# A gated linear recurrence followed by a cosine-gated two-layer block: TensorE's order fixed by hand, transposes and x through DRAM, weights on GpSimd's queue, first groups closer together

## The chip, the cores and the metric

One core of one Trainium2 chip. The metric is device time in microseconds (us) of one execution. Every kernel was run on the same chip as the kernel before in the same rounds. The rounds ran on several chips, where the kernel before took 821.0 to 823.5 us in the median, so times of different rounds compare only to some 3 us; the ratios to the kernel before don't have this fault. The time of a single instruction comes from the one profiled run of each kernel.

Words used below: TensorE (PE in the profile), VectorE (DVE), ScalarE (ACT), GpSimd (POOL), SyncE (SP; its queue is SPq). "hp" is the first matrix product of the gated block, "op" the second; "lgs" and "phs" are running sums over a chunk (of logarithms and of phases); "sc", "sp" and "yp" are the scores, the states and the attention outputs. A number in brackets is the group: hp(0), lgs(3). A "record" is one matmul instruction in the trace; the "span" is the time from the first to the last instruction of the profiled run.

## The reference

```python
# q, k, v, a_re, a_im: (4, 8, 768, 48) float32; w_in (384, 2048), w_out (2048, 384): float64
mag = sqrt(a_re**2 + a_im**2);  scale = minimum(mag, 0.999) / (mag + 1e-6)
for t in range(768):                                   # complex gate a, state S of 48 x 48
    S = a[t] * S + outer(k[t], v[t])
    y[t] = q[t] @ real(S)
x = y, heads side by side                              # (3072, 384)
h = x @ w_in
out = (h * cos(h)) @ w_out                             # (3072, 384) float32
```

## The kernel before

The recurrence is done in 24 chunks of 128 steps, two chunks to a group, 12 groups. For each group: logarithms of the gate, their running sums (lgs) and exponentials; angles by arctangent, their running sums (phs), sine and cosine; keys and queries multiplied by these and transposed; then sc, sp, yp; then x is brought to the layout that hp wants, and the gated block follows. Work of four groups is woven: `weave` gives every piece a place between 0 and 1 and emits the pieces in that order. The weights come as float64 and are put together from their bits on chip.

```python
def from_double(dst, src):                 # 28 times: 12 pieces of w_in, 16 of w_out
    nc.sync.dma_start(out=raw, in_=src)
    nc.vector.tensor_scalar(...)           # L595: shift and mask of the upper word
    nc.vector.scalar_tensor_tensor(...)    # L597: sign
    nc.scalar.activation(out=low, ...)     # lower word
    nc.gpsimd.tensor_tensor(out=bits, in0=bits, in1=low, op=ALU.add)
    nc.vector.tensor_scalar(out=e, ...)    # L601, L603: range check of the exponent
    nc.scalar.activation(out=e, ...)
...
def f_transpose(n, name):                  # one chunk; 32 x 32 blocks, then 12 small moves
    nc.vector.transpose(out=tr, in_=...)
    for a in range(Q4):
        for b in range(NR):
            nc.sync.dma_start(out=place[ts(b, 32), a], in_=tr[ts(a, 32), b])
...
for it in range(NG + 3):
    g, c, m, o = it, it - 1, it - 2, it - 3
    ...g_log(g); g_prod(g); g_angle(g)...
    ...mm2(o, i) for both chunks...                                  # op
    weave((gates(g), 0.0, 0.5), (chunks(c), 0.0, 1.0), (weights.get(it, ()), 0.0, 1.0),
          ([mm1(m, jp) for jp in range(NJ // 2)], 0.0, 1.0))         # hp
```

TensorE's instructions are ordered by the scheduler; only ScalarE's table functions are chained by hand.

Of the kernel before, what the change touches and what calls it, by code (L numbers as in the profile page):

```python
# [485 lines left out]
def fast_path(ctx, tc, q, k, v, a_re, a_im, moe_w_in, moe_w_out, out, least, odd):  # L486
# [16 lines left out]
    R = 16  # L503
    NR = D // R
    Q4 = C // 32
    NJ = DF // C
# [31 lines left out]
    def load(g, names):  # L538
        for name in names:
            ap = {"re": a_re, "im": a_im, "q": q, "k": k, "v": v}[name]  # L540
            X[g][name] = ld.tile([C, G, H, D], F32, tag=name, name=name,
                                 bufs=2 if name == "v" else 1)
            for i in range(G):
                b, c = divmod(g * G + i, NCH)
                nc.sync.dma_start(  # L545
                    out=X[g][name][:, i],
                    in_=ap[b].rearrange("h (c p) d -> p c h d", p=C)[:, c])

    load(0, ("re", "im", "k", "q", "v"))
# [15 lines left out]
    def weight_parts():  # L565
        wi = moe_w_in.rearrange("(c p) f -> p c f", p=C)
        wo = moe_w_out.rearrange("(j p) e -> p j e", p=C)
        parts = [(w_in[:, c, ts(i, W)], wi[:, c, ts(i, W)])
                 for i in range(DF // W) for c in range(ND)]
        parts += [(w_out[:, j], wo[:, j]) for j in range(NJ)]  # L570
        return [lambda dst=dst, src=src: weight(dst, src) for dst, src in parts]
# [7 lines left out]
    def from_double(dst, src):  # L579
# [8 lines left out]
        raw = stage.tile([C, n], I64, tag="raw", name="raw")  # L588
        nc.sync.dma_start(out=raw, in_=src)
# [3 lines left out]
        e = stage.tile([C, n], U32, tag="e", name="e", bufs=1)  # L593
# [6 lines left out]
        nc.gpsimd.tensor_tensor(out=bits, in0=bits, in1=low, op=ALU.add)  # L600
        nc.vector.tensor_scalar(out=e, in0=hi, scalar1=1, scalar2=21,  # L601
# [11 lines left out]
    chained = []  # L613

    def chain(ins):
        if chained:
            tc.add_manual_dep(ins.ins, chained[-1].ins.name, mybir.DependencyInfo(
                mybir.DependencyClass.NoSync, mybir.DependencyReason.DATA))
        chained.append(ins)
# [17 lines left out]
    def g_log(g):  # L637
# [3 lines left out]
        re, im = flat(x["re"]), flat(x["im"])  # L641
        m2, sq, rs, mag = temp("m2"), temp("sq"), temp("rs"), temp("mag")
# [13 lines left out]
        nc.gpsimd.tensor_tensor(out=m2, in0=m2, in1=rs, op=ALU.subtract)  # L656
        x["lg"] = m2
        nc.gpsimd.tensor_tensor(out=mag, in0=mag, in1=sq, op=ALU.mult)  # L658
# [4 lines left out]
        x["tan"] = sq  # L663

    def g_prod(g):


        x = X[g]
        x["P"], x["Q"] = temp("P"), temp("Q")
        for i in range(G):  # L670
            ps = pa.tile([C, DM], F32, tag="a", name="lgs")
            nc.tensor.matmul(ps, lhsT=sums, rhs=x["lg"][:, ts(i, DM)], start=True, stop=True)  # L672
            special(out=x["P"][:, ts(i, DM)], in_=ps, func=AF.Exp)
            special(out=x["Q"][:, ts(i, DM)], in_=ps, func=AF.Exp, scale=-1.0)
        u = temp("mag")
        nc.vector.scalar_tensor_tensor(out=u, in0=x["Q"], scalar=HUGE, in1=x["P"],
                                       op0=ALU.min, op1=ALU.mult)
        for name in "PQ":
            nc.vector.scalar_tensor_tensor(out=x[name], in0=u, scalar=3.0, in1=x[name],
                                           op0=ALU.subtract, op1=ALU.mult)  # L680
        row = rows_d.tile([G * DM], F32, tag="row", name="row")
        nc.scalar.dma_start(out=row, in_=x["P"][C - 1:C].rearrange("o x -> (o x)"))
        x["end"] = ft.tile([D2, G * H], F32, tag="end", name="end")
        for part in range(D2 // R):
            nc.sync.dma_start(
                out=x["end"][ds(part * R, R)],
                in_=row.rearrange("(x b d) -> b d x", d=R, b=NR)[part // 2])
        nc.vector.tensor_scalar(out=x["end"], in0=x["end"], scalar1=-0.5, scalar2=None,
                                op0=ALU.mult)
        nc.vector.scalar_tensor_tensor(out=least, in0=x["end"], scalar=LEAST, in1=least,  # L690
                                       op0=ALU.is_ge, op1=ALU.min)

    def g_angle(g):
        x = X[g]
        at, fl = x["tan"], temp("rs")
        special(out=at, in_=at, func=AF.Arctan)
        nc.scalar.activation(out=fl, in_=at, func=AF.Identity, scale=-2.0 / math.pi, bias=half_b)  # L697
        nc.vector.scalar_tensor_tensor(out=fl, in0=flat(x["re"]), scalar=0.0, in1=fl,
# [3 lines left out]
        x["turn"] = at  # L702
        x["ph"] = temp("ph", 2)

    def g_phase(g, i):
        x, n = X[g], g * G + i
        ps = pa.tile([C, DM], F32, tag="a", name="phs")
        first = n % NCH == 0
        nc.tensor.matmul(ps, lhsT=sums, rhs=x["turn"][:, ts(i, DM)], start=True, stop=first)  # L709
        if not first:  # L710
            prev = X[(n - 1) // G]["ph"][:, ts((n - 1) % G, DM)]
            nc.tensor.matmul(ps, lhsT=last, rhs=prev, start=False, stop=True)  # L712
        ph = x["ph"][:, ts(i, DM)]
# [4 lines left out]
    def g_trig(g):  # L718
        x = X[g]
        cs, sn = x["trig"] = temp("rs"), temp("mag")  # L720
        nc.vector.tensor_scalar(out=cs.bitcast(U32), in0=x["ph"].bitcast(U32),
                                scalar1=0x7FFFFFFF, scalar2=None, op0=ALU.bitwise_and)
        special(out=sn, in_=x["ph"], func=AF.Sin, scale=TWO_PI)
        special(out=cs, in_=cs, func=AF.Sin, scale=-TWO_PI, bias=half_pi_b)

    def g_stack(g):
        x = X[g]
        nc.gpsimd.tensor_tensor(out=x["P"], in0=flat(x["q"]), in1=x["P"], op=ALU.mult)
        nc.gpsimd.tensor_tensor(out=x["Q"], in0=flat(x["k"]), in1=x["Q"], op=ALU.mult)  # L729
        for name, src in (("ks", x["Q"]), ("qs", x["P"])):  # L730
            t = gt.tile([C, G * H * NR, 2, R], F32, tag=name, name=name,
                        bufs=2 if name == "ks" else 1)
            for a in range(2):
                nc.vector.tensor_tensor(
                    out=t[:, :, a], in0=src.rearrange("p (x d) -> p x d", d=R),
                    in1=x["trig"][a].rearrange("p (x d) -> p x d", d=R), op=ALU.mult)
            x[name] = t

    def f_transpose(n, name):


        g, i = divmod(n, G)
        tr = ft.tile([C, NR, H, 32], F32, tag="tr", name="tr")
        nc.vector.transpose(out=tr, in_=X[g][name[0] + "s"][:, ts(i, H * NR)].rearrange(
            "p (h b) a d -> p b h (a d)", b=NR))
        if name == "kT":
            t = Y[n][name] = ft.tile([D2, H, Q4, 32], F32, tag=name, name=name, bufs=3)
            place = t.rearrange("p h q j -> p q h j")
        else:
            t = Y[n][name] = place = ft.tile([D2, Q4, H, 32], F32, tag=name, name=name, bufs=3)  # L750
        for a in range(Q4):
            for b in range(NR):
                nc.sync.dma_start(out=place[ts(b, 32), a], in_=tr[ts(a, 32), b])  # L753

    def queries(y, h):
        return y["qT"][:, :, h]

    def f_scores(n, hh):
# [4 lines left out]
        for h in range(HH):  # L763
            nc.tensor.matmul(ps[:, h], lhsT=y["kT"][:, hh * HH + h], rhs=queries(y, hh * HH + h),  # L764
                             start=True, stop=True)
# [3 lines left out]
    def f_out(n):  # L769
# [6 lines left out]
        for p in range(HH):  # L776
            for side in range(2):
                nc.tensor.matmul(ps[ds(side * 64, D), p], lhsT=vals[:, 2 * p + side],  # L778
                                 rhs=y["atm"][:, 2 * p + side], start=True, stop=(state is None))
            if state is not None:  # L780
                for side in range(2):
                    nc.tensor.matmul(ps[ds(side * 64, D), p], lhsT=state[:, 2 * p + side],  # L782
                                     rhs=queries(y, 2 * p + side), start=False, stop=True)
# [4 lines left out]
    def f_state(n):  # L788
# [4 lines left out]
        for h in range(H):  # L793
            keys = X[g]["ks"][:, ts(i * H + h, NR)].rearrange("p b a d -> p (b a d)")
            nc.tensor.matmul(ps[:, h], lhsT=keys, rhs=X[g]["v"][:, i, h], start=True, stop=True)  # L795
# [11 lines left out]
    def f_xt(g):  # L807

        xt = X[g]["xT"] = msb.tile([C, ND, G, C], F32, tag="xT", name="xT")
        for h in range(H):  # L810
            row = h * D
            while row < (h + 1) * D:
                n = min((h + 1) * D, (row // C + 1) * C) - row
                nc.sync.dma_start(out=xt[ds(row % C, n), row // C],
                                  in_=X[g]["yT"][ds(h % 2 * 64 + row - h * D, n), h // 2])
                row += n

    def mm1(g, jp):
        x = X[g]
        ps = pm.tile([C, 2, G * C], F32, tag="m", name="hp")  # L820
        for ji in range(2):
            for dc in range(ND):
                nc.tensor.matmul(ps[:, ji], lhsT=w_in[:, dc, ts(jp * 2 + ji, C)],  # L823
                                 rhs=x["xT"][:, dc].rearrange("p g t -> p (g t)"),
                                 start=(dc == 0), stop=(dc == ND - 1))
# [137 lines left out]
```

## Time and profile before

| | before |
|---|---|
| time | 821.39 us, median of 3 runs (820.37 to 822.25) |
| TensorE busy before 200 us | 96.9 us (414 records), clock 0.74 |
| TensorE busy from 200 to 823 us | 600.2 us (3052 records), clock 1.00 |
| first hp | 128.5 us |

The table has two rows of busy time because the profile has two regimes, and only the first has much to win. Busy time alone misleads in it: at half clock the same matmul is twice as long (16 sc records take 3.75 us at 75 us, where the granted clock from 74 to 79 us is 0.50, and 1.79 at 347 us, at 1.00). So the text below counts TensorE's work as *floor work*: the number of records times the duration of one at full clock. The whole kernel is 656 us of it.

### The profile page before, as it was taken

How to read it: one execution, taken by the hardware profiler on the slowest of the kernel's cores; microseconds unless marked ns; L12 is line 12 of the kernel's file. 1: busy time of each engine (PE TensorE's matmuls, PEld its weight loads, DVE VectorE, ACT ScalarE, POOL GpSimd, SP SyncE). 2: the span in 40 equal slices, each digit the busy share in tenths (PEclk: the TensorE clock that was granted, in tenths of full speed). 3: DMA queues.
4: the chain of work that ended last, by engine and by line, in shares of the span. 5: the costliest groups of instructions: out<-in, count | busy, mean ns of one | idle time of the engine just before them, and what ended most of it. 6: DMA issues, size and time to landing. Idle time of an engine off the chain costs nothing.

```text
span 823.1 us, 10293 instructions
## 1 busy us (share of the span) xinstructions
PE 697.1 (85%) x3464; PEld 514.9 (63%) x3464; DVE 488.7 (59%) x754; ACT 376.4 (46%) x576; POOL 146.6 (18%) x96
## 2 busy tenths in 40 slices
PE   1217286766899999999999989999999999999997
PEld 0006174534575785876867857858758668677674
DVE  2876454957685574864954856757658458234060
ACT  5552615663666345453571562464545624123140
POOL 1341124322401113003012021040040120000000
PEclk9956576897999999999999999999999999999999
DMA  9624257545632722623625427226236231210000
GB/s 178 128 47 71 45 128 192 129 103 115 164 80 49 150 45 62 119 49 68 112 51 92 84 49 135 42 54 123 49 62 110 51 73 30 49 40 21 20 0 23
DMA packets 251481, 65.67 MB, mean 80 GB/s; under 512 B 230414, under 2 KB 247823, under 8 KB 251419
## 3 DMA queue, kind: packets, MB, share of 16 engines
q1 hardware_dynamic: 250818, 64.62, 38.6%
q8 instruction: 29, 0.48, 0.3%
q10 hardware_dynamic: 600, 0.30, 0.2%
q14 instruction: 34, 0.27, 0.1%
HBM read 36.51 MB, written 4.76 MB: 50 GB/s over the span
## 4 chain that ended last, share of the span: by engine, by line
PE 53%; SPq 15%; DVE 12%; ACT 9%; issue 4%; DMA 3%; POOL 3%; DVEq 0%; ACTq 0%; POOLq 0%
PE hp L823 20%; PE op L841 18%; SPq L753 12%; PE sc L764 3%; ACT rs L629 2%; PE lgs L672 2%; POOL m L656 2%; PE phs L709 2%; PE yp L778 2%; PE sp L795 2%; DVE gate L833 2%; PE phs L712 1%; PE yp L782 1%; ACT L628 1%; SPq L545 1%
## 5 line engine op out<-in xcount | busy, mean ns | idle before, releaser
L823 PE MATMUL hp<-xT,w_in 128*128 128x256 f32 x1152 | 272.9, 390 | 16.0 <-DMA xT<-yT 8.6
L841 PE MATMUL op<-w_out,gate 128*128 128x384 f32 x768 | 256.3, 490 | 17.3 <-POOL w_out L600 17.1
L823 PEld LDWEIGHTS hp<-xT,w_in 128*128 128x128 f32 x1152 | 218.4, 194 | 53.1 <-DVE gate L835 8.7
L841 PEld LDWEIGHTS op<-w_out,gate 128*128 128x128 f32 x768 | 145.8, 191 | 118.5 <-POOL w_out L600 21.3
L829 ACT ACTIVATE turn<-hp,quarter_b 128x512 f32<-128x512 f32 x96 | 65.5, 683 | 91.4 <-PE hp L823 90.2
L629 ACT ACTIVATE gate<-gate 128x512 f32<-128x512 f32 x96 | 60.2, 628 | 102.4 <-DVE gate L833 102.3
L835 DVE TENSOR_TENSOR gate<-hp,gate 128x512 f32<-128x512 f32 x96 | 65.5, 685 | 38.8 <-ACT gate L629 38.4
L831 DVE TENSOR_SCALAR gate<-turn 128x512 f32<-128x512 f32 x96 | 40.7, 427 | 61.9 <-ACT turn L829 61.0
L672 PE MATMUL lgs<-m,sums 128*128 128x384 f32 x48 | 25.1, 657 | 52.2 <-POOL m L656 52.2
L833 DVE TENSOR_TENSOR gate<-turn,gate 128x512 f32<-128x512 f32 x96 | 67.2, 702 | 1.7
L801 POOL TENSOR_TENSOR state<-state,end 96x384 f32<-96x384 f32 x16 | 16.8, 1050 | 266.2 <-DVE state L799 175.2
L844 ACT ACTIVATE ot<-op 128x384 f32<-128x384 f32 x24 | 11.6, 484 | 114.4 <-PE op L841 114.4
L764 PEld LDWEIGHTS sc<-qT,kT 96*128 96x128 f32 x384 | 53.0, 206 | 15.6 <-issue 9.8
L764 PE MATMUL sc<-qT,kT 96*128 96x128 f32 x384 | 53.5, 290 | 7.4 <-issue 4.1
L656 POOL TENSOR_TENSOR m<-m,rs 128x768 f32<-128x768 f32 x12 | 21.7, 1808 | 178.0 <-ACT rs L629 178.0
L672 PEld LDWEIGHTS lgs<-m,sums 128*128 128x128 f32 x48 | 10.6, 245 | 64.7 <-POOL m L656 59.8
L714 DVE TENSOR_SCALAR ph<-phs 128x384 f32<-128x384 f32 x24 | 13.3, 555 | 55.7 <-PE phs L712 40.8
L709 PE MATMUL phs<-sq,sums 128*128 128x384 f32 x48 | 23.0, 570 | 27.2 <-DVE sq L700 27.2
L766 DVE TENSOR_TENSOR atm<-sc,causal 128x512 f32<-128x512 f32 x48 | 32.6, 682 | 18.8 <-PE sc L764 18.6
L659 DVE SCALAR_TENSOR_TENSOR sq<-mag,sq 128x768 f32<-128x768 f32 x12 | 11.5, 958 | 49.1 <-POOL mag L658 49.1
L778 PE MATMUL yp<-atm,v 128*48 128x128 f32 x384 | 38.2, 288 | 0.0
L729 POOL TENSOR_TENSOR Q<-k,Q 128x768 f32<-128x768 f32 x12 | 25.6, 2130 | 55.8 <-ACT rs L697 19.7
(75 smaller groups left out, 812.6 us busy)
## 6 DMA issues: line engine op xcount, KB each, us to landing
kT<-tr SPq DMA_DIRECT2D x288, 32.0 KB, 2.0
qT<-tr SPq DMA_DIRECT2D x288, 32.0 KB, 1.8
raw<-in_moe_w_in_dram SPq DMA_DIRECT2D x12, 512.0 KB, 4.8
raw<-in_moe_w_out_dram SPq DMA_DIRECT2D x16, 384.0 KB, 3.8
re<-in_a_re_dram SPq DMA_DIRECT2D x24, 192.0 KB, 3.0
im<-in_a_im_dram SPq DMA_DIRECT2D x24, 192.0 KB, 4.1
k<-in_k_dram SPq DMA_DIRECT2D x24, 192.0 KB, 4.0
q<-in_q_dram SPq DMA_DIRECT2D x24, 192.0 KB, 4.6
```

Source lines behind the costliest of these rows:

```text
L629: chain(nc.scalar.activation(func=func, **kw))
L672: nc.tensor.matmul(ps, lhsT=sums, rhs=x["lg"][:, ts(i, DM)], start=True, stop=True)
L709: nc.tensor.matmul(ps, lhsT=sums, rhs=x["turn"][:, ts(i, DM)], start=True, stop=first)
L753: nc.sync.dma_start(out=place[ts(b, 32), a], in_=tr[ts(a, 32), b])
L764: nc.tensor.matmul(ps[:, h], lhsT=y["kT"][:, hh * HH + h], rhs=queries(y, hh * HH + h), start=True, stop=True)
L778: nc.tensor.matmul(ps[ds(side * 64, D), p], lhsT=vals[:, 2 * p + side], rhs=y["atm"][:, 2 * p + side], start=True, stop=(state is None))
L823: nc.tensor.matmul(ps[:, ji], lhsT=w_in[:, dc, ts(jp * 2 + ji, C)], rhs=x["xT"][:, dc].rearrange("p g t -> p (g t)"), start=(dc == 0), sto ...
L829: nc.scalar.activation(out=turn, in_=ps, func=AF.Identity, scale=INV_TWO_PI / in_scale, bias=quarter_b)
L831: nc.vector.tensor_scalar(out=cs, in0=turn, scalar1=ROUND, scalar2=ROUND, op0=ALU.add, op1=ALU.subtract)
L833: nc.vector.tensor_tensor(out=cs, in0=turn, in1=cs, op=ALU.subtract)
L835: nc.vector.tensor_tensor(out=gate, in0=ps, in1=cs, op=ALU.mult)
L841: nc.tensor.matmul(ps, lhsT=X[g]["gate"][j // 2][:, j % 2, ts(i, C)], rhs=w_out[:, j], start=(j == 0), stop=(j == NJ - 1))
```

## The change

The intent is to let TensorE start its dense work sooner. Each group's transposes go through DRAM in two large hops (7 issues instead of 48), x likewise (3 instead of 10); group 0 is done in two halves; the weights are issued by GpSimd, and the range check of the weights is moved out of the start to a second read of them ("re-reads"); TensorE's matmuls are chained in the order of the program; and the first three groups get a weave of their own. Cut to its core:

```diff
+    def matmul(out, **kw):
+        chain(nc.tensor.matmul(out, **kw), "tensor")
...
-        nc.sync.dma_start(out=raw, in_=src)
+        nc.gpsimd.dma_start(out=raw, in_=src)
...
+    def guard(src):                        # the range check, on a second read of the weights
+        nc.sync.dma_start(out=raw, in_=src)
...
-        for a in range(Q4):
-            for b in range(NR):
-                nc.sync.dma_start(out=place[ts(b, 32), a], in_=tr[ts(a, 32), b])
+        nc.sync.dma_start(out=moved..., in_=tr)
+        if name == "kT":
+            for q4 in range(Q4):
+                nc.sync.dma_start(out=X[g][name][:, ds(i * H, n * H), q4], in_=moved[q4])
+        else:
+            nc.sync.dma_start(out=X[g][name][:, :, ds(i * H, n * H)], in_=moved...)
...
+    weave((each(g_log, 0), 0.0, 0.2), (prods(0), 0.2, 0.4), (angles(0), 0.4, 0.5),
+          (phases(0), 0.5, 0.6), (keys(0), 0.6, 1.0), (convert(into[:6]), 0.2, 1.0))
+    weave((chunks(0), 0.0, 0.4), (each(g_log, 1), 0.0, 0.1), (convert(into[6:]), 0.0, 0.4),
+          (prods(1), 0.4, 0.41), (angles(1), 0.42, 0.5), (phases(1), 0.7, 0.8), (first(0), 0.4, 1.0),
+          (convert(back), 0.4, 1.0))
+    weave((keys(1), 0.0, 0.1), (each(g_log, 2), 0.1, 0.2),
+          (second(0), 0.0, 0.8), (prods(2), 0.4, 0.42), (angles(2), 0.42, 0.5),
+          (phases(2), 0.75, 0.9), (chunks(1), 0.4, 0.95))
+    for it in range(3, NG + 3):
+        g, c, m, o = it, it - 1, it - 2, it - 3 if it > 3 else -1
+        weave((keys(c), 0.0, 0.08), (each(g_log, g), 0.08, 0.1), (second(o), 0.0, 0.36),
+              (prods(g), 0.36, 0.38), (angles(g), 0.38, 0.42), (phases(g), 0.6, 0.72),
+              (chunks(c), 0.45, 0.95), (first(m), 0.36, 1.0), (re-reads, 0.1, 0.9))
```

Two more edits: the logarithms' tile `lg` is now also the product P of its group, with one buffer; and GpSimd's multiplications of group 0 go to VectorE. Smaller ones: the tile `raw`, into which the weights are loaded, has four buffers instead of two, and the gates have twelve instead of eleven.

## The prediction

> **What bounds the kernel now.** I read the page first (busy shares, then the 40 slices, then the groups), after that the table of stretches, the chain of waits, the issue queue of SyncE and the timeline of the start.
>
> From the page:
>
> ```profile
> PE 697.1 (85%) x3464; PEld 514.9 (63%) x3464; DVE 488.7 (59%) x754; ACT 376.4 (46%) x576; POOL 146.6 (18%) x96
> PE   1217286766899999999999989999999999999997
> PEclk9956576897999999999999999999999999999999
> L823 PE MATMUL hp<-xT,w_in 128*128 128x256 f32 x1152 | 272.9, 390 | 16.0 <-DMA xT<-yT 8.6
> ```
>
> TensorE is busy 85% of 823.1 us, and the slices say where the other 15% is: from the tenth slice on (about 200 us) it is full, before that it is mostly idle and its granted clock is 0.5 to 0.8. So there are two regimes, and the table of stretches puts sizes on them (columns: length, then busy time of PE, PEld, DVE, ACT, POOL, clock, DMA share, GB/s):
>
> ```profile
> 0.00:20.00 20.00, 2.93 (x4) 1.17 (x4) 4.97 (x15) 10.76 (x15) 3.77 (x6) 1.00 1.07 184
> 40.00:60.00 20.00, 2.93 (x4) 1.18 (x4) 15.19 (x21) 13.18 (x21) 7.30 (x5) 0.50 0.23 44
> 80.00:100.00 20.00, 7.76 (x44) 5.45 (x43) 7.09 (x9) 12.33 (x17) 4.40 (x3) 0.50 0.34 61
> ...
> 350.00:400.00 50.00, 48.93 (x261) 35.98 (x262) 30.52 (x46) 24.94 (x36) 9.57 (x5) 1.00 0.47 87
> 750.00:800.00 50.00, 50.00 (x219) 36.76 (x218) 18.80 (x31) 15.69 (x25) 0.00 (x0) 1.00 0.06 17
> ```
>
> After 200 us the stretches add up to 600.2 us of TensorE work in 617 us (its last matmul ends at 817): 17 us idle in all. Before 200 us it is busy 96.9 us, much of it at half clock. The prize is at the start.
>
> What does TensorE need at full clock? From the chain of waits in the steady part:
>
> ```profile
> 282.51 2.66 PE hp L823 x12
> 290.75 2.59 PE hp L823 x12
> 293.35 1.32 PE sp L795 x16
> 346.69 1.79 PE sc L764 x16
> 755.13 20.64 PE op L841 x64
> ```
>
> So one hp record is 2.59/12 = 0.216 us, op 20.64/64 = 0.3225, sc 1.79/16 = 0.112, sp 1.32/16 = 0.0825. The timeline gives 1.97 us for the yp of a chunk with a state, 1.01 without, 0.65 for a pair of phs records, 1.56 for four lgs. Times counts: hp 1152: 248.6; op 768: 247.7; sc 384: 43.0; sp 320: 26.4; yp 20 x 1.97 + 4 x 1.01: 43.4; phs 88: 28.6; lgs 48: 18.7. **Sum 656 us**: the floor that the change does not touch, as it adds and removes no matmul. 823 - 656 = 167 us is what can be won, about 20 of it after 200 us, the rest in the start.
>
> Why is the start slow? SyncE issues the transposes' moves in order, and its timeline shows:
>
> ```profile
> 41.84 7.98 SPq L753 DMA_DIRECT2D kT<-tr  x12
> 49.92 7.53 SPq L753 DMA_DIRECT2D qT<-tr  x12
> 65.50 7.86 SPq L753 DMA_DIRECT2D qT<-tr  x12
> 79.86 8.29 SPq L753 DMA_DIRECT2D kT<-tr  x12
> 122.20 2.35 SPq L814 DMA_DIRECT2D xT<-yT  x3
> ```
>
> Each set of 12 costs 7.5 to 8.3 us of issue (0.65 each). Group 0 alone needs 48, 31 us; xT of group 0 is ready to go once yT is copied at about 86 us, but stands behind group 1's 48 issues until 122. The first hp runs at 128.5, and then waits for weights, xT and gates until 200.
>
> [...] 16 sc records take 3.75 us at 75 us, clock 0.50, against 1.79 later. [...] in the trace lgs waits 11.9 us for POOL after 200 us, with ready op matmuls queued behind. [...] the 32 KB moves here land in a median 1.8 to 2.0 us. [...] VectorE's L601 takes 0.42 us alone, 1.47 and 2.03 beside a GpSimd operation. No run yet has DMAs from GpSimd.
>
> **The change part by part.**
>
> (1) *Transposes through DRAM.* 48 issues a group become 2 writes and 5 reads: 7 (14 in group 0, done in halves). At 0.65 us that takes 34 x 0.65 = 22 us of issue off group 0 and 41 x 0.65 = 27 off each later group. [...] For a full group 786 KB each is written and read for k and for q. At the 187 GB/s of the 192-byte loads in the first 14 us, the kT read alone (128-byte pieces) is 4 to 6 us. Estimate for stack to last landing in a full group: 15 to 18 us, hidden if TensorE has 21 us of op in front.
>
> (2) *x through DRAM*: 10 issues a group become 3, one hop more; 5 to 6 us either way, but no queue of 48 in front.
>
> (3) *Weights on GpSimd's queue*, range check (e, L601 and L603) moved off the conversion to later re-reads: takes per weight 0.42 us of VectorE, 0.9 us of ScalarE and the SyncE issue out of the start. GpSimd has 12 x 1.34 + 16 x 1.18 = 35 us of conversion (rows of L600), its group-1 products about 8 [...] converted by about 90 us, when op of group 0 wants w_out. The re-reads, 4 a group later, are 0.3% or so of DMA each and off the path.
>
> (4) *Halves and first groups closer.* Walk of group 0 in the order of the changed queues, with half-width costs of the rows (ScalarE 0.48, VectorE 0.51, less when pipelined): VectorE's queue has the conversion of the first three weights ahead of group 0's third step, so it cannot pass until weight 3 has landed; at 184 GB/s, 1.6 MB of weights beside 0.8 MB of re and im is 13 to 15 us. From there (14): logs and products to 25, phs of half 0 at 27, trig and stack to 36, transposes 38.5, two hops to 46; half 1 follows in VectorE's queue to 45, landing 52; sc, sp, yp of it at half clock to 63, yT 65, x and xT by 70, the estimate of (2). **First hp at about 72** (with 2 for waits that I missed), against 128.5, and it then runs dense. 14 us of floor work lies before it.
>
> (5) *Fixed order, op first in an iteration.* From 72: hp of group 0, op of its first half, then sc of group 1 waits for keys(1), whose phases are only in the second half of hp(0): about 7 us lost. Then lgs(3) waits for the logs that come after keys(2) on ScalarE: about 12, and sc(2) 5 more. From the fourth iteration 64 op records (20.6 us) hide logs and keys, and lgs no longer waits for POOL (11.9 us saved), but sc may wait 0 to 3 us for kT: say 1.8 x 8 = 14. Clock losses after the gaps 4. Sum of bubbles 42.
>
> Total: 72 + (656 - 14) + 42 + 6 (the tail after the last matmul, 817 to 823, unchanged) = 762. I think my walk is a little pessimistic, since the weave fractions look tuned, and put down **757 us**.
>
> **Rivals.** (a) *GpSimd becomes the bound of the start*: [...] op(0) waits, and the time is 785 to 800. For: L600 was released late in before (op waits 17.1 us for it)[...]. [...] (b) *Double hop too slow in steady state*: 5 us a group waiting on kT or qT would add 30: about 785. For: 3.1 MB a group through DRAM; against: DMA is at 0.4 share there and 21 us of op precede. (c) *Nothing lost at all*: bubbles of 15 and first hp at 65 give 728. (d) *Transfers were hidden anyway*: the time stays near 820. Against: the chain of waits gives SyncE's queue 15% of the span, and PE's slices are empty just there.
>
> **Range and chances.** 757 with (c) below and (a), (b) above: 734 to 786 in 8 of 10. Slower than 805 (2%) would need (a) and (b) together: faster 0.95, within 2% 0.04, slower 0.01.
>
> **What would show it.** Right: first hp between 65 and 80 us; slices full from the fifth; PE busy near 680 to 690 (less half-clock work); SyncE's share of the chain near zero; lgs waiting for POOL gone in the steady part. Wrong: op(0) waiting for w_out from POOL (a); sc waiting on kT or qT beyond 3 us a group (b); gaps at the third iteration above 25 us, or a clock below 0.9 after 120 us.

## The result and the profile after

The changed kernel is correct and takes **789.72 us** (median of 4 runs, 788.54 to 791.51) against 820.97 (4 runs) of the kernel before in the same rounds; the ratio is 0.962, with a 95% interval of 0.959 to 0.964. Ratios here are the mean time of one kernel's fast runs over that of the other's of the same rounds, so not quite the ratio of the medians quoted. The gain is 31 us, half of the 64 that were forecast, and the time lies above the range. The profiled run, 791.51 us, has a span of 789.6; times read from the trace belong to this span.

From the page of the changed kernel (busy times, some of the rows of 40 slices of 19.7 us each, and the group of hp):

```profile
PE 684.7 (87%) x3464; PEld 512.0 (65%) x3464; DVE 521.6 (66%) x757; ACT 375.8 (48%) x589; POOL 151.2 (19%) x120
...
PE   0337585682999999999999999999999999999996
...
DVE  4889897646876776677668667668676675443150
...
PEclk9999788695999999999999999999999999999999
DMA  9897868998739339259275274293492631711000
...
L631 PE MATMUL hp<-xT,w_in 128*128 128x256 f32 x1152 | 267.0, 385 | 15.0 <-DMA xT<-x 8.7
```

TensorE is full from the eleventh slice, hardly sooner than before. VectorE and the DMA engines, 61% and 53% busy in the first 200 us of the kernel before (122.8 us, and a share of 0.53), are at 76% and 85% in the first 206 here, and VectorE is nearly always busy from 40 to 120 us (73.0 of 80 us). The table of stretches (columns as in the prediction):

```profile
0.00:20.00 20.00, 1.65 (x2) 0.50 (x2) 9.15 (x25) 10.29 (x20) 5.02 (x10) 1.00 0.95 226
40.00:60.00 20.00, 6.52 (x36) 6.39 (x38) 17.47 (x26) 10.35 (x13) 8.98 (x8) 1.00 0.96 246
...
80.00:100.00 20.00, 9.91 (x36) 8.12 (x36) 17.34 (x21) 7.54 (x13) 16.20 (x17) 0.76 0.80 223
...
350.00:400.00 50.00, 50.00 (x272) 38.53 (x271) 34.73 (x52) 27.06 (x40) 9.12 (x5) 1.00 0.59 117
```

In the stretch 40 to 60 us VectorE goes from 15.2 to 17.5 us busy and the DMA engines from 0.23 to 0.96; at 350 us TensorE goes from 48.9 to 50.0 of 50 us. The steady part became nearly full (573.3 of the 583 us after 206 us); the start did not. The spans differ by 33.5 us. TensorE's idle time after about 200 us falls from 17 to 8.6 us, so by this estimate some 8 us were won there and some 25 in the start.

SyncE's issues of the first half of group 0 (start, length):

```profile
41.35 1.41 SPq L776 DMA_DIRECT2D moved<-tr  x2
43.95 2.74 SPq L779 DMA_DIRECT2D kT<-moved  x4
46.79 0.58 SPq L781 DMA_DIRECT2D qT<-moved  x1
```

These 4.7 us, for k and q of one chunk, answer to two sets of 12 before, 15.5 us. SyncE no longer spends the start on issuing small moves, as intended. (Its share of the chain of waits reads 1% instead of 15%, but the chain on the new page reaches back only to 451 us, so it says nothing about the start.)

Where TensorE stands (start, length, instruction, and in brackets how long it had been idle and for what):

```profile
84.98 9.91 PE L631 MATMUL hp<-xT,w_in 128*128 128x256 f32 x36 [8.75 <-DMA xT<-x]
101.10 5.20 PE L631 MATMUL hp<-xT,w_in 128*128 128x256 f32 x12 [6.21 <-DVE gate L867]
...
141.68 2.93 PE L631 MATMUL lgs<-lg,sums 128*128 128x384 f32 x4 [11.62 <-POOL lg L679]
147.06 2.05 PE L631 MATMUL sc<-qT,kT 96*128 96x128 f32 x8 [2.46 <-DMA qT<-moved]
...
169.07 0.88 PE L631 MATMUL phs<-tan,sums 128*128 128x384 f32 x2
...
191.53 2.93 PE L631 MATMUL lgs<-lg,sums 128*128 128x384 f32 x4 [17.56 <-POOL lg L679]
...
247.17 1.45 PE L631 MATMUL lgs<-lg,sums 128*128 128x384 f32 x4
```

The first hp runs at 85 us. Then come four stalls, at 95 (gates), 130 (lgs(2)), 145 (sc(1)) and 174 (lgs(3)): 37.9 us in all. After lgs(3) there is next to none.

**One sum that carries the rest.** In all kernels in which I counted it (the changed one, e3, e9, f1, f4 and g2 below), 72.5 to 72.9 us of floor work are done when lgs(3) starts, so 583 are left. The span is then the time of lgs(3), plus 583, plus 6 for the tail, plus what is lost later. Here: 191.5 + 583.5 + 6 = 781, and the span is 789.6: **8.6 us lost in 598.** So the question is what puts lgs(3) at 191.5. (f1 will show that the cut belongs one group later, at lgs(4). In the changed kernel nothing is lost between the two: 55.6 us for some 55 us of floor work.)

### The profile page after: what moved, and what is told of

Its sections match the earlier page's. It is cut to its first block, busy times and chain, and to the rows that moved or that the text cites. A ratio compares the mean times of both kernels' runs of the same rounds, so it can differ in the third digit from the quotient of the medians.

```text
span 789.6 us, 9472 instructions
## 1 busy us (share of the span) xinstructions
PE 684.7 (87%) x3464; PEld 512.0 (65%) x3464; DVE 521.6 (66%) x757; ACT 375.8 (48%) x589; POOL 151.2 (19%) x120
## 5 line engine op out<-in xcount | busy, mean ns | idle before, releaser
L631 PE MATMUL hp<-xT,w_in 128*128 128x256 f32 x1152 | 267.0, 385 | 15.0 <-DMA xT<-x 8.7
L631 PE MATMUL op<-w_out,gate 128*128 128x384 f32 x768 | 252.7, 490 | 0.0
L641 ACT ACTIVATE gate<-gate 128x512 f32<-128x512 f32 x96 | 60.4, 629 | 153.7 <-DVE gate L865 153.6
L865 DVE TENSOR_TENSOR gate<-turn,gate 128x512 f32<-128x512 f32 x96 | 79.6, 829 | 1.5
L679 POOL TENSOR_TENSOR lg<-lg,rs 128x768 f32<-128x768 f32 x11 | 20.3, 1845 | 268.3 <-ACT rs L641 266.0
L631 PE MATMUL lgs<-lg,sums 128*128 128x384 f32 x48 | 22.8, 602 | 48.2 <-POOL lg L679 29.2
L879 ACT ACTIVATE ot<-op 128x384 f32<-128x384 f32 x24 | 11.8, 490 | 90.3 <-PE op L631 90.3
L832 POOL TENSOR_TENSOR state<-state,end 96x384 f32<-96x384 f32 x16 | 16.9, 1054 | 171.3 <-DVE state L830 121.5
L631 PEld LDWEIGHTS lgs<-lg,sums 128*128 128x128 f32 x48 | 10.4, 229 | 56.8 <-POOL lg L679 30.4
L681 DVE SCALAR_TENSOR_TENSOR tan<-mag,tan 128x768 f32<-128x768 f32 (+1 forms) x13 | 11.6, 895 | 38.5 <-POOL mag L680 38.4
L599 ACT ACTIVATE low<-raw,carrier_b 128x384 uint32<-128x384 uint32 (+1 forms) x28 | 19.2, 691 | 34.1 <-DMA raw<-in_moe_w_out_dram 12.7
L817 ACT COPY yT<-yp 48x512 f32<-48x512 f32 x48 | 27.5, 574 | 14.7 <-PE yp L631 14.2
L631 PEld LDWEIGHTS sp<-v,ks 128*96 128x96 f32 x320 | 32.5, 176 | 1.2 <-issue 0.2
```

The lines of the kernel that those rows point to most:

```text
L599: nc.scalar.activation(out=low, in_=lo, func=AF.Identity, scale=2.0 ** -29, bias=carrier_b)
L631: chain(nc.tensor.matmul(out, **kw), "tensor")
L641: chain(nc.scalar.activation(func=func, **kw))
L679: mult.tensor_tensor(out=m2, in0=m2, in1=rs, op=ALU.subtract)
L817: nc.scalar.copy(out=X[g]["yT"][half, :, i], in_=ps[half])
L832: nc.gpsimd.tensor_tensor(out=new, in0=new, in1=end, op=ALU.mult)
```

## The experiments

The first suspects were the re-reads, GpSimd's queue and the fixed order of TensorE. A check of each alone:

**e1**: no re-reads (a kernel without the range check).

```diff
-          ([lambda: guard(guards.pop(0)) for _ in range(min(per, len(guards)))], 0.1, 0.9))
+          ([lambda: guards.pop(0) for _ in range(min(per, len(guards)))], 0.1, 0.9))
```

> The changed kernel without its range-check re-reads (28 loads of 512 or 384 KB and their 28 operations on VectorE and ScalarE taken out; the check then passes trivially, the output stays right). Theory T1, the start is short of DMA: these re-reads are hoisted to 100-175 us, where the DMA share is 0.83 to 0.95, so without them the gap of 11.6 us before lgs of group 2 and of 17.6 us before lgs of group 3 shrink by some 5 us each and the time is 775 to 781. Rival T2, TensorE's fixed order holds ready matmuls behind lgs: the gaps stay, 786 to 790. T3, GpSimd's queue paces the weights: no change before 120 us in any of the two, 786 to 790.

Measured: 794.49 us (ratio 0.966, 0.963 to 0.970), lgs(3) at 192.8. The edit also moved the scheduler's order of the start (first hp at 91.8), so it isn't a clean removal, but the 12.6 MB fewer brought nothing. T1 missed.

**e2**: the re-reads held to their place in the program. The scheduler had hoisted them to 100 to 175 us.

```diff
-        nc.sync.dma_start(out=raw, in_=src)
+        ...the same issue, with an order (no wait) after the newest issue of SyncE before it
```

> All re-reads kept, but each held on SyncE's queue behind the transfer that the program names just before it, so that four come in each group from the fourth iteration on, as the prediction had assumed. T1: as e1 (775 to 781), as the placing and not the bytes costs. T2 and T3: 786 to 790. If e1 gains and this doesn't, the work itself costs.

Measured: 790.45 us (0.963, 0.958 to 0.968). lgs(3) comes 6 us sooner, at 185.4, but 3.5 of these 6 us are lost again later: 601.6 us of the span lie after lgs(3), instead of 598.1. The profiled run is also the fastest of the four (788.75 us); the median shows no gain.

**e3**: the weights issued by SyncE, as before.

```diff
-        nc.gpsimd.dma_start(out=raw, in_=src)
+        nc.sync.dma_start(out=raw, in_=src)
```

> The changed kernel with the 28 weight loads issued by SyncE instead of GpSimd. T3 (weights wait for GpSimd's turn: raw is loaded only after the conversion in front of it on the same in-order queue): first hp a few us earlier or the 6.2 us stall in hp of group 0 gone, 780 to 785. T1: the same bytes over the same engines at the same time, 786 to 794. T2: 788 to 791.

Measured: 791.15 us (0.962, 0.959 to 0.964). The first lgs comes at 10.1 instead of 16.9, the first hp at 76.7 instead of 85.0: GpSimd's queue costs the start 8 us. Yet lgs(3) moves only from 191.5 to 187.9, and the time not at all. Something later than the first hp takes the 8 us back: at lgs(4), 247.0 against 247.2, nothing is left of them.

**e4**: TensorE's order left to the scheduler again.

```diff
-        chain(nc.tensor.matmul(out, **kw), "tensor")
+        nc.tensor.matmul(out, **kw)
```

> The changed kernel without the dependency chain over matmuls; the scheduler then puts all 27 of the op matmuls before lgs of group 2 and 19 hp before lgs of group 3 and sc of group 2. T2: most of the two gaps (11.6 and 17.6 us) is filled, 770 to 778, and the clock stays up. T1 and T3: the work moved forward is missed later, when sc waits for its operands anyway: 786 to 795.

Measured: 789.58 us (0.960, 0.957 to 0.963), within 0.3% of the changed kernel. The waits ahead of lgs fall to 3.6 and 2.2 us and other waits come instead (7.2 for xT(1), 4.3 for a gate). phs(2) comes at 159.7 instead of 169.1 and lgs(3) at 181.9, both some 10 us sooner, and the median is the same. (The profiled run, 784.15 us, is the fastest of the four.) The order fixed by hand is neither the gain nor the fault as a whole.

So no single suspect. The next four tested whether VectorE's load in the start (T4) or the transfers (T5) bind it.

**e5**: the two VectorE instructions of every conversion left out (wrong).

```diff
-        nc.vector.tensor_scalar(out=bits, in0=hi, ...)
-        nc.vector.scalar_tensor_tensor(out=bits, in0=hi, ...)
-        nc.gpsimd.tensor_tensor(out=bits, in0=bits, in1=low, op=ALU.add)
+        nc.gpsimd.tensor_tensor(out=bits, in0=low, in1=low, op=ALU.add)
```

> Wrong on purpose: the two VectorE instructions of every weight conversion (44 us of VectorE between 30 and 120 us of the changed kernel, some 20 us of it waiting inside the instruction) are left out; the loads, ScalarE's step and GpSimd's add stay. Theory T4 (the start is bound by the serial work of VectorE and ScalarE, the conversions above all): hp(0) starts by 78 instead of 85, lgs(3) comes at 170 to 178 instead of 191.5, and the time falls to 768 to 778 (ratio to the kernel before 0.935 to 0.947). Rival T5 (transfers and their queues bind each group's chain): hp(0) at 83 to 86, lgs(3) at 187 to 192, time 785 to 791 (0.955 to 0.963).

Measured: 790.39 us (0.960, 0.956 to 0.963); lgs(3) at 185.0, hp(0) *later*, at 88.1. T4 falls in this form. With VectorE's two steps out of the way the DMA engines move 262 and 286 GB/s instead of 193 and 246 in the two stretches from 20 to 60 us, and their share goes to 1.00 and 1.04 from 0.85 and 0.96; sc(0) waits for its transposes until 57.3 instead of 51.9, although VectorE ends the transposes of that half 2 us sooner (40.4 against 42.4). The likely reading, which no run shows apart, is that a slow engine had been holding back transfers that now get in the way.

**e6**: GpSimd's add replaced by an OR on VectorE (relative error 0.52: the result is wrong; the steady part shows no trace of it: after 260 us hp and op take a mean of 380 and 486 ns here and in the changed kernel).

```diff
-        nc.gpsimd.tensor_tensor(out=bits, in0=bits, in1=low, op=ALU.add)
+        nc.vector.tensor_tensor(out=bits, in0=bits, in1=low, op=ALU.bitwise_or)
```

> GpSimd's add of the conversion is replaced by an OR on VectorE (24 or so more instructions there of some 0.35 us each, 10 us, and GpSimd has nothing left of the conversion); the rounding's carry is lost, so the result may be slightly off. If half of VectorE's 44 us are waits beside GpSimd, the groups of VectorE's two conversion lines fall from means of 0.85 to 1.18 us to about 0.4 to 0.55, the sum of the three from 44 to 35 or less, and the time falls by 3 to 10 us (780 to 787). If the waits have another cause (the shape, the clock, the transfers), the means stay above 0.8 and the time rises by 3 to 8 us (793 to 798).

Groups of the conversion's first VectorE line, in the changed kernel and then in e6 (busy us, mean ns):

```profile
L595 DVE TENSOR_SCALAR w_out<-raw 128x384 uint32<-128x384 uint32 x16 | 13.8, 868 | 3.2 <-DMA raw<-in_moe_w_out_dram 3.2
...
L595 DVE TENSOR_SCALAR w_in<-raw 128x512 uint32<-128x512 uint32 x12 | 11.8, 988 | 9.6 <-DMA raw<-in_moe_w_in_dram 9.6
```

```profile
L595 DVE TENSOR_SCALAR w_out<-raw 128x384 uint32<-128x384 uint32 x16 | 5.5, 353 | 2.9 <-DMA raw<-in_moe_w_out_dram 2.9
...
L595 DVE TENSOR_SCALAR w_in<-raw 128x512 uint32<-128x512 uint32 x12 | 4.9, 418 | 6.2 <-DMA raw<-in_moe_w_in_dram 6.2
```

The first line of the conversion runs 2.4 times as long when GpSimd does the add (868 against 353 ns, 988 against 418): 15 of its 26 us are gone in e6. The second line only goes from 23.0 to 20.7 us, and the OR costs 19.6, so VectorE has nothing left of it, and the time is 790.81 us (0.961, 0.956 to 0.966), lgs(3) at 187.3. That VectorE's line is longer with GpSimd's add in the program is shown; that this sets the time is not.

**e7**: a second buffer for `lg` (one fewer for the gates, to fit).

```diff
-                x[name] = temp(name, 2 if name == "tan" else 1)
+                x[name] = temp(name, 2 if name in ("tan", "lg") else 1)
-        gate = ...bufs=12)
+        gate = ...bufs=11)
```

> The logarithms' tile gets a second buffer (it is also the product P of the group before), with one gate buffer fewer to make room. Theory T4b (the next group's logarithms wait for the keys of the group before through this one buffer): the wait of lgs(3) of 17.6 us falls to under 9, the interval from lgs(2) to lgs(3) from 50 to about 42, and the time to 780 to 784 (0.950 to 0.955). Rival (VectorE's queue order holds them in the same place, since the next group's logarithms stand behind the transposes there anyway): the wait falls by less than 4 us and the time stays within 787 to 791.

Measured: 791.55 us (0.962, 0.959 to 0.966). The wait of lgs(3) falls from 17.6 to 13.9 us, and the interval from lgs(2) to lgs(3) stays at 49. The rival is right: the buffer isn't what holds them.

**e8**: the blocks moved from SBUF to SBUF in one hop, 24 issues of 64 KB for k and q of a full group.

```diff
-        nc.sync.dma_start(out=moved..., in_=tr)
-        ...the reads of `moved`...
+        for a in range(Q4):
+            for b in range(NB):
+                nc.sync.dma_start(out=place[ts(b, 32), a, ds(i * H, n * H)], in_=tr[ts(a, 32), b])
```

> The 32 x 32 blocks go from SBUF to SBUF in one hop and 24 small issues per half or group, instead of through DRAM in two hops and 7 issues. T5 (the two hops bind the start): from the transpose to sc(0) 9.5 us become 6 to 7, sc(1) of half 1 comes at 56 to 59 instead of 63.9, hp(0) at 77 to 80, and the time falls by 5 us or more. T4: the hop is not what ends last, the start gains 0 to 4 us at sc(0) and the time stays within 786 to 794, with the 24 issues at some 0.7 us each (17 us) eating the saved hop on SyncE.

Measured: 839.29 us (1.018, 1.015 to 1.022), with sc(0) at 59.6 and lgs(3) at 205.1, and after 206 us sc waits another 23 us in ten places. Both theories missed this by 45 us or more. The two hops through DRAM, slow as they are, are worth some 50 us against this way of going direct. That the change's gain comes from them is likely but not shown: the kernel before also went direct, with other blocks and orders, so the two are not the same by subtraction.

Then the profile itself gave a theory. ScalarE's table functions are a fixed order too (start, length):

```profile
124.48 0.61 ACT L641 ACTIVATE gate<-gate 128x512 f32<-128x512 f32 x1
125.00 0.82 ACT L641 ACTIVATE sin<-tan 128x768 f32<-128x768 f32 x1
...
147.00 0.84 ACT L641 ACTIVATE tan<-tan 128x768 f32<-128x768 f32 x1
...
175.48 0.83 ACT L641 ACTIVATE sin<-tan 128x768 f32<-128x768 f32 x1
```

and on VectorE, the end of the angles of group 2:

```profile
151.33 2.44 DVE L726 SCALAR_TENSOR_TENSOR tan<-tan,rs 128x768 f32<-128x768 f32 x1
```

The angles of group 2 are ready at 153.8, but TensorE's fixed order has their phs behind the work of group 1, at 169.1. From there: the sine at 175.5, the keys, and only behind these the logarithms of group 3, so lgs(3) at 191.5. In the same way the sine of group 1, whose argument VectorE had finished at 115.6, stands behind the last gate of hp(0) until 125.0, and lgs(2) comes 16.7 us after it. **T6: the fixed orders of ScalarE and TensorE make one serial chain of the first three groups**, and it starts where hp(0) ends. VectorE, whose order is the scheduler's, is a link of it too: its first step for the logarithms of group 3 runs at 184.0, right behind the transposes of keys(2).

**e9**: no weights at all (wrong).

```diff
+    nc.gpsimd.memset(w_in, 0.37)
+    nc.gpsimd.memset(w_out, 0.23)
...
-            from_double(dst, src)
+            pass                           # and no re-reads, as in e1
```

> Wrong on purpose: no weights are loaded or converted or read again (both weight tiles are filled with a constant by GpSimd), so the start has neither their transfers nor their VectorE, ScalarE and GpSimd work. Theory T6 (the fixed orders bind the start: the keys of group 1 stand behind all gates of hp(0) on ScalarE, the phases of group 2 behind chunks(1) on TensorE, and the logarithms of group 3 behind the keys of group 2): hp(0) starts at 62 to 72 and takes 21 to 26 us, but the interval from lgs(2) to lgs(3) stays 44 to 50 us, lgs(3) comes at 158 to 170 and the time is 756 to 770, far from the 40 us or more that a start free of weights should give. Rival (weights' transfers and conversions bind the whole start): the interval falls under 38 us, lgs(3) comes before 150, and the time is under 750.

```profile
110.63 2.93 PE L633 MATMUL lgs<-lg,sums 128*128 128x384 f32 x4 [8.06 <-POOL lg L681]
...
160.19 2.93 PE L633 MATMUL lgs<-lg,sums 128*128 128x384 f32 x4 [16.84 <-POOL lg L681]
```

Measured: 764.58 us (0.928, 0.924 to 0.933). First hp at 66.6, lgs(2) at 110.6, lgs(3) at 160.2: the interval is 49.6 us, as it was with the weights. Two things follow. The weights, transfers and work of the engines together, cost 25 us (28 by the ratios). And even a start without any weights is slower than the prediction.

**e10**: the phases of groups 1 and 2 sooner in the weave.

```diff
-          ...(phases(1), 0.7, 0.8)...
+          ...(phases(1), 0.5, 0.55)...
-          (phases(2), 0.75, 0.9), ...
+          (phases(2), 0.5, 0.6), ...
```

> Only the places of two lists in the weave change: the phases of group 1 at 0.50 to 0.55 instead of 0.7 to 0.8 and those of group 2 at 0.5 to 0.6 instead of 0.75 to 0.9, so that TensorE's fixed order has them sooner. T6: phs(2) comes within 6 us of its angles (which are ready at 153.8 in the changed kernel, while phs(2) stands until 169), the interval from lgs(2) to lgs(3) falls from 50 to 34 to 40, lgs(3) comes at 174 to 182, and the time is 775 to 783 (ratio 0.943 to 0.953). Rival (VectorE, GpSimd or the transfers bind the chain anyway): lgs(3) moves by less than 5 us and the time stays 786 to 792.

```profile
105.06 1.62 PE L631 MATMUL phs<-tan,sums 128*128 128x384 f32 x2 [16.13 <-DVE tan L726]
```

Measured: 797.01 us (0.970, 0.967 to 0.972). The interval falls to 35.7 us, as T6 says, but its lgs(3), 183.8, and its time are missed: phs(1) now stands *ahead* of its operand, and hp(0) behind it waits 16 us: the loss is my edit's. lgs(2) slides to 148.1.

**e11**: the next group's logarithms ahead of the keys, in every iteration (with the buffers of e7).

```diff
-        weave((keys(c), 0.0, 0.08), (each(g_log, g), 0.08, 0.1), ...
+        weave((each(g_log, g), 0.0, 0.01), (keys(c), 0.01, 0.1), ...
```

> In the third weave and in every later one the logarithms of the next group go ahead of the keys of the group before, on ScalarE and VectorE; the logarithms' tile gets a second buffer for it and the gates one fewer. T6: lgs(3) no longer waits for phs(2): it comes at 160 to 172 and stops being the stall ahead of hp(1), which then waits for xT(1) and starts at 178 to 185; the time is 776 to 785. Rival: the wait moves to sc(2) or hp(1) in full and the time stays 786 to 793.

```profile
PE sc L631 <- DMA qT<-moved: 131.7, 13, 23.1
```

(us waited in all, times, longest.) Measured: 899.85 us (1.095, 1.092 to 1.099), a plain miss. The keys then come late in every group, and sc waits for qT 13 times. As an order for all groups, the change's order of these two is the better one.

**e12**: e10 and e11 together, and the keys of group 1 inside the second weave.

```diff
+          ...(phases(1), 0.5, 0.55), (keys(1), 0.6, 0.7)...
-    weave((keys(1), 0.0, 0.1), (each(g_log, 2), 0.1, 0.2),
+    weave((each(g_log, 2), 0.0, 0.1),
```

> The phases of both groups early, the keys of group 1 already inside the second weave instead of behind all gates of hp(0), and the next group's logarithms ahead of the keys. T6: lgs(2) at 122 to 132 instead of 141.7, lgs(3) at 155 to 170, hp(1) at 165 to 176, and the time 765 to 776 (ratio 0.930 to 0.944). Rival (the chain is bound by engines and transfers): the time stays above 783, with the same us found as waits of sc(1), hp(0) for gates, or xT(1).

Measured: 892.89 us (1.087, 1.083 to 1.091), e11's loss again. lgs(2) at 146.2 and lgs(3) at 180.1 miss T6's 122 to 132 and 155 to 170 as well.

The last six separate the steps, each on top of the one before. (f1 is e10 without moving the phases of group 1.)

**f1**: only the phases of group 2.

```diff
-          (phases(2), 0.75, 0.9), ...
+          (phases(2), 0.5, 0.6), ...
```

> Only the phases of group 2 move, to 0.5 to 0.6 of the third weave. T6: lgs(2) stays at 139 to 144, phs(2) comes at 150 to 157 instead of 169, the interval from lgs(2) to lgs(3) is 34 to 38 us, lgs(3) at 174 to 181, and hp(0) shows no stall for tan; the time is 778 to 785. Rival (what is saved is given back to waits for qT and xT, as these moves then run beside each other and beside the re-reads): sc(2) waits 6 us or more for qT and the time stays 786 to 791.

```profile
154.05 0.81 PE L631 MATMUL phs<-tan,sums 128*128 128x384 f32 x2
...
178.00 2.93 PE L631 MATMUL lgs<-lg,sums 128*128 128x384 f32 x4 [4.97 <-POOL lg L679]
183.35 4.57 PE L631 MATMUL hp<-xT,w_in 128*128 128x256 f32 x12 [2.43 <-DMA xT<-x]
194.36 2.04 PE L631 MATMUL sc<-qT,kT 96*128 96x128 f32 x8 [6.45 <-DMA qT<-moved]
...
247.23 1.45 PE L631 MATMUL lgs<-lg,sums 128*128 128x384 f32 x4
```

phs(2) comes 15 us sooner, the wait of lgs(3) falls from 17.6 to 5.0, and lgs(3) comes at 178.0, all as T6 says. But the time is 792.34 us (0.962, 0.961 to 0.964): by the sum, 178.0 + 583 + 6 leaves 24.6 us of later losses instead of 8.6. The two waits of hp(1) and sc(2) above are 9 of them, and 5 more are the half clock after them (12 hp, 8 sc and 12 hp records take 4.57, 2.04 and 4.88 us; the page's slice from 178 to 198 us has 5 tenths of the clock). At lgs(4) the trace is level with the changed kernel again, 247.23 against 247.17. The reason stands on VectorE: the sine comes 12 us sooner (163.1), but VectorE now runs the logarithms of group 3 (from 168.2) ahead of the last products of keys(2) (173.0), so its transposes start only 4 us sooner (175.9 against 179.8). What lgs(3) won, the keys lost. Mechanism of T6, outcome of the rival.

So lgs(3) is one group too early as the cut. What is left of the span after lgs(3) is 598.1 to 613.7 us in sixteen kernels (all but e8, e11 and e12, whose edits slow every group); after lgs(4) it is 541.5 to 547.2.

**f2**: f1, and more of hp(1) ahead of sc(2).

```diff
-              (chunks(c), 0.45, 0.95), (first(m), 0.36, 1.0),
+              (chunks(c), *((0.45, 0.95) if it > 3 else (0.65, 0.98))), (first(m), 0.36, 1.0),
```

> The step before, and chunks(2) at 0.65 to 0.98 of the fourth weave instead of 0.45 to 0.95, so that more of hp(1) lies ahead of sc(2). T6: sc(2) waits under 2 us and the time is 3 to 6 us below the step before (774 to 781). Rival: hp(1) itself waits for xT(1) and the time is within 2 us of the step before.

Measured: 788.36 us (0.958, 0.956 to 0.961), 4 us less than f1: the wait for qT is gone, and lgs(4) comes at 237.8, but the level lies above what I expected.

**f3**: f2, and the keys of group 1 in the second weave, ahead of the last gates of hp(0), instead of at the head of the third.

```diff
-          ...(phases(1), 0.7, 0.8)...
+          ...(phases(1), 0.7, 0.8), (keys(1), 0.85, 0.95)...
-    weave((keys(1), 0.0, 0.1), (each(g_log, 2), 0.1, 0.2),
+    weave((each(g_log, 2), 0.0, 0.1),
```

> The step before, and the keys of group 1 at 0.85 to 0.95 of the second weave, ahead of the last gates of hp(0), instead of behind them all. T6: the sine of group 1 comes at 116 to 119 instead of 125, lgs(2) at 133 to 137 instead of 141.7, and the time is 4 to 8 us below the step before (768 to 776). Rival: the gates it delays stop hp(0) or op(0) by as much, and the time is within 2 us of the step before.

Measured: 783.95 us (0.955, 0.951 to 0.959), 4 us less; lgs(2) at 139.5, lgs(3) at 176.6. The sine comes at 118.9, as T6 says, but its 133 to 137 for lgs(2) is missed: two gates now stop op(0) for 3 us. Its interval overlaps that of f2, so this step alone is likely, not certain.

**f4**: f3, and the weights on SyncE.

```diff
-        nc.gpsimd.dma_start(out=raw, in_=src)
+        nc.sync.dma_start(out=raw, in_=src)
```

> The step before, and the weights on SyncE's queue, which brought hp(0) forward by 8 us and the time by nothing when done alone. T6: with the orders mended the 8 us count: hp(0) at 75 to 79, lgs(3) 5 to 8 us earlier than in the step before, time 5 to 8 us below it. Rival (the start is bound elsewhere, by transfers): within 2 us of the step before.

Row of TensorE in the slices of f4; its first ten slices hold 54 tenths, those of the changed kernel above 47:

```profile
PE   1246865778999999999999999999999999999996
```

Measured: **777.63 us** (0.945, 0.941 to 0.949), correct. First hp at 76.2, lgs(3) at 172.3. The 8 us of e3, worth nothing alone, are worth 6 here; lgs(3) gains 4 of the 5 to 8 that were expected. This is the best correct version, 12 us below the changed kernel (14 by the ratios).

**g1**: f4 with the re-reads held to their place (the diff is e2's).

> f4 with the re-reads held to their place in the program. If their bytes lengthen the moves of x and q at 165 to 200 us in f4 (xT(1) lands 11.8 us after its last yp there), the hop falls to 8 to 10 us, lgs(3) comes 2 to 5 us earlier and the time is 770 to 776. If not, or if later groups pay for the re-reads as they did when this was done alone, the time is 776 to 784.

Measured (6 runs): 779.84 us (0.948, 0.946 to 0.951). lgs(3) comes 2.5 us sooner and later groups pay for it, as in e2. The re-reads are not the cause, placed early or late.

**g2**: f3's orders without weights (wrong; the diffs are f1's, f2's, f3's and e9's).

> Wrong on purpose: no weights loaded, converted or read again, under the orders of f3. If orders and weights are two causes that add (weights 25 us as in e9, orders 6 us as in f3): hp(0) at 64 to 70, lgs(3) at 142 to 150, and the time 750 to 760. If the orders only mattered because weights crowded the start: the time is 762 or more, as in e9.

Measured: 753.78 us (0.917, 0.914 to 0.921); first hp at 66.7, lgs(2) at 109.7, lgs(3) at 146.1. Side by side, time and (lgs(3); lgs(4)):

| | orders of the change | orders of f3 |
|---|---|---|
| weights on GpSimd's queue | 789.7 (191.5; 247.2) | 784.0 (176.6; 236.6) |
| weights on SyncE's queue | 791.2 (187.9; 247.0) | 777.6 (172.3; 232.1) |
| no weights | 764.6 (160.2; 217.0) | 753.8 (146.1; 205.8) |

In each row the mended orders bring lgs(3) forward by 14 to 16 us and the time by 6 to 14; in each column taking the weights away brings 24 to 30 us (23 to 31 by the ratios). Weights and orders are two causes that add: to within 2 us at lgs(3), 4 at lgs(4) and 8 in the time. With the weights gone and the orders mended the time is 754, near what was predicted. That is no proof of the walk: it had counted something for both (weights that land at 14 us, 23 us of bubbles), and it had the first hp at 72 and lgs(3) at 153.6, where g2 has 66.7 and 146.1.

## Why the prediction was wrong

Use the sum. The walk's 762, less 6 for the tail, 583.4 of work left and the 19 us of bubbles forecast after lgs(3) (14 in the steady part and 5 before sc(2)), put lgs(3) at 153.6. It came at 191.5, 38 us later; the later losses were 8.6 instead of 19, 10 us less. 762 + 38 - 10 is 789.6 to within the rounding. The 5 us taken off by feeling ("I think my walk is a little pessimistic") went the wrong way.

- **What bounds the kernel: right.** The start was the prize, and SyncE's queue of small moves was in its way; e8, which brings small moves back in another form, is 50 us slower. One reading was off: TensorE is full from the twelfth slice on (226 us), not the tenth.
- **Step (4), first hp at 72: the step that failed first**, by 13 us. phs(0) came at 31.1, not 27; two hops took 10.5 us (41.4 to 51.9), not 7.5; the second half's sc came at 63.9, not 52; x took 8 us to come, not 5 or 6. e3 assigns 8 of the 13 us to the weights on GpSimd's queue.
- **Step (5), the bubbles from the first hp to lgs(3): the step that failed most.** The forecast was 7 + 12 + 4 for the clock, 23 us. Lost were 106.5 us less 58.3 of floor work, 48: 6.2 for gates (not in the list at all), 14.1 ahead of lgs(2) and sc(1), 17.6 ahead of lgs(3), and some 10 at half clock (granted 0.51 from 100 to 106 us, 0.55 from 141 to 155). The prediction named the places and gave each the size of one wait. It did not see that they are one serial chain through the engines' orders; T6's runs (e9, e10, f1) show this by its interval, 50 us with and without weights, 36 with phs(2) moved. (The 5 us forecast at sc(2) did not come.)
- **Step (3): right that GpSimd would not hold op(0)** (no wait for w_out there), wrong that taking the range check away relieves VectorE. Its two conversion lines went from 30.3 us in all to 48.6 (40.3 in e3), which eats the 17.4 of the check. (At the prediction's 0.42 us each the check would be 11.8.) e6 shows GpSimd's side of it. GpSimd's issues took some 0.55 us each (medians 0.545 and 0.554); that the weights would be converted by 90 us was the estimate. And e5 shows that this load, taken away alone, does not move the time either.
- **"The re-reads are off the path": right in effect** (e1, e2, g1), wrong in place: they ran at 100 to 175 us and not spread over later groups.
- **Step (1): a figure for the transfers.** The 187 GB/s for the first 14 us reads 173 in the trace (187 from 1 to 14 us); the estimate for kT, 4 to 6 us, came true all the same (4.8 and 5.0 us median in e3 and f4).
- **The steady part: better than forecast.** After 206 us sc waits 3.0 us for qT in all, and lgs no longer waits for GpSimd. Rival (b) did not come. Rival (a) came in another form: the weights cost 25 us in the start (e9), without op(0) ever waiting for w_out.
- **The signs that it named** told it well: first hp outside 65 to 80, the slices full from the eleventh instead of the fifth, the clock at 0.66 and 0.63 in the stretches 140 to 160 and 180 to 200 us, all on the side of wrong. Busy time of 684.7 and lgs no longer waiting for GpSimd were on the side of right. The sign of gaps above 25 us at the third iteration did not show: lgs(2) and sc(1) wait 14.1 us there, and the longest gap comes one iteration later. SyncE's 1% is of little weight, as its chain doesn't reach the start.

Left open: what x through DRAM, the halves of group 0 and the new weave bring by themselves, and so which part brings most of the 31 us; and how the 25 us of the weights split between transfers and engines, as e5 and e6 each traded one for the other.

## What to carry to other kernels

When several engines have orders fixed by hand, look for an operand that is ready long before its reader runs: the reader is behind something in its own queue. Moving it ahead of its operand stops everything behind it (16 us in e10), and moving it rightly pays only as far as the next wait (in f1 lgs(3) comes 13.5 us sooner and lgs(4) no sooner). Find the one instruction after which the work left is the same in all versions and the pipeline is full (here lgs(4); lgs(3) was one group too early), forecast *its* time by walking the chain of every engine's order, and count a gain at an earlier point as nothing until it has reached that one. And relieving an engine in a crowded start can save nothing: in e5 the DMA share went to 1.04 and the first hp came 3 us later.

## What the traces show of the transfers, of VectorE beside GpSimd, and of the orders

- Medians from issue to landing: the small moves of the kernel before, of 16 to 48 KB, take 1.8 to 2.0 us. In f4 the 768 KB that the change writes to DRAM take 3.7, the 768 KB of qT that are read back 6.8, and 192 KB of kT, in pieces of 128 bytes, 5.0. The five reads of a group are in flight together, and no run separates what the pieces cost from what the company costs.
- The first VectorE line of the conversion takes 868 ns for a piece of w_out with GpSimd's add in the program, and 353 without it (e6). The 28 weight loads from GpSimd's queue land in a median of 4.7 us, the longest in 8.8, with VectorE 89% busy from 20 to 120 us (89.4 of 100 us). By size it is 6.2 us for 512 KB and 4.1 for 384; from SyncE's queue in e3, where the re-reads count with them, 5.1 and 4.0. Most of the 8 us that e3 wins are there at the first lgs, at 16.9 and 10.1. What differs before it is the order of the first transfers: GpSimd issues three w_in pieces at 1.3 us, and the first of them is converted at 8.1; in e3 the first is converted at 19.8.
- Orders fixed on several engines add up to one chain across groups: 50 us from lgs(2) to lgs(3), 36 with one list moved.
